# A fused attention and mixer kernel: stores of r two ticks later, five w2 tiles spread over the second pass, words of the head's conversions at other places

## The chip, the cores and the metric

The kernel runs on one core of one Trainium2 chip. The metric is the device time of one execution in microseconds; lower is better. All times of before come from three timed runs and from one profiled execution.

## What is computed

The reference is a linear attention with decay, whose output x (4 batches, 768 positions, 512 columns) goes through a low-rank mixing over positions and a two-layer channel product:

```python
h = xt @ U @ V                                     # xt = x transposed, rank 32
u = x + h.transpose(0, 2, 1)
ch = np.maximum(u @ w_ch1, 0.0) @ w_ch2            # 512 -> 2048 -> 512
return (u + ch).astype(np.float32)
```

The attention walks over blocks of 64 positions with a 64x64 state for each of 32 heads. The change does not touch it. The weights U, V, w_ch1 and w_ch2 come as 64-bit numbers, that is as pairs of 32-bit words; the kernel makes fp32 numbers of them.

## The kernel before, in words

The work runs in five parts. TensorE multiplies numbers in the form fp32r, which keeps fewer bits than fp32, so every operand is split into a high and a low part, and a product is made of three matmuls: high by high and low by low (or a near relative of these) into one accumulator, and a third with sums of the parts into another or the same one, with scales that bring the pieces together.

1. **The attention** for 24 blocks of 128 positions, with its products, the low-rank mixing and the transposes into columns u.
2. **The head of the first product** (`hidden`, lines 889 to 906): four units, each a pair of groups of 512 rows by one tile of 128 of the 2048 hidden columns. A unit has 16 matmuls of high and low parts, 8 of the third part, two evacuations by ScalarE (L896), two sums by VectorE (L905) and two stores of r (L906). Between its matmuls other pieces are placed by number: `(unit, n, what)` means "ahead of matmul n of this unit". Among them are mixings (`mix`, whose sum x_nat is L626), transposes of the last six blocks (`turn`, L659), and the steps that convert words to weights.
3. **The single units** (`run_unit`): the first four groups by the other tiles, with 8 + 4 matmuls each. Beside them run the conversions of w1 and w2 tiles, strewn over the units by tables (`strew`: this step after that unit). Sums and differences of w1 halves are made here and stored as `forms_d`.
4. **The second pass** of the first product: the last two groups. For the tile pairs 1 to 7 it multiplies seven forms instead of eight (`seven_of`, a scheme of Strassen's kind); pair 0 takes the plain eight (`eight_of`). Its order is `sequence`, 53 forms; after the high pieces of a form stands a `tick`, at which the steps strewn over the tick numbers run. A block of seven ticks belongs to one pair. A form takes six matmuls. The weights come as a stream: for every two forms a load of `forms_d` (L1088), the high part on ScalarE (L276), the low part on VectorE (L279), the third on GpSimd (L285). Results r are taken from the accumulators by ScalarE (L1197), summed by VectorE (L1193) and stored by `give` (L1201).
5. **The second product**: relu(r) is split into three parts m (`split`, L1306 ScalarE, L1307 and L1308 VectorE) after a load (`fetch`, L1300), and multiplied with the 16 tiles of w2 (L1322, L1324, L1326). A w2 tile is prepared by `w2_split` with the steps load, high, low, third. The first four tiles get their own buffers (`e`) and are made during the second pass, with the third part on GpSimd; the others are made at the beginning of the second product, with low (L267) and third (L270) on VectorE, into buffers that the first product has left.

What sets the order: each engine takes its instructions in program order, and up to the end of the second pass that order is written out by hand (`manual_schedule`); what follows `ordered.close()` is placed by the framework, and may begin between the last pieces of the second pass. All loads and stores of the parts 2 to 5 are issued by one queue, SP, which waits in its order, too: a store that waits for a sum holds the loads behind it.

Converting a tile of w1 has eight steps: fetch the words (L149; one buffer in the head, three later), `one` (L170 on VectorE, then L177 and L178 on ScalarE), `two` (L188), `three` (L196, the last reader of the words), `four` (L201), `five` (L231, ScalarE), `six` (L234) and `seven` (L239, both VectorE). In the head `second` and `third` are these steps for the w1 tiles 2 and 3.

Of the kernel before, what the change touches and what calls it, by code (L numbers as in the profile page):

```python
# [18 lines left out]
def kernel(  # L19
# [28 lines left out]
    nc = tc.nc  # L48
# [7 lines left out]
    FT = FF // P  # L56
# [46 lines left out]
    r_d = [[dram.tile([P, N], FP32, name=f"r_d{ft}_{g}") for g in range(NG)] for ft in range(FT)]  # L103
    w2_d = [dram.tile([P, C], FP32, name=f"w2_d{ft}") for ft in range(FT)]
    forms_d = [dram.tile([P, 8, C // 2], FP32, name=f"forms_d{j}") for j in range(FT // 2)]
# [119 lines left out]
    def w1_steps(ft, in_parts=False, apart=False):  # L225
        st = {}

        def five():
            w1v[ft] = o = w_tile(ft)
            st["t"], st["p"] = o[:, 0, :].bitcast(FP32), w1_plain[ft]  # L230
            on_scalar(lambda: nc.scalar.mul(o[:, 0, :], st["p"], NEAR))  # L231

        def six():
            nc.vector.tensor_tensor(  # L234
                out=w1v[ft][:, 1, :], in0=st["p"], in1=st["t"], op=ALU.subtract
            )

        def seven():
            nc.vector.scalar_tensor_tensor(  # L239
                w1v[ft][:, 2, :], st["t"], -E, w1v[ft][:, 1, :].bitcast(FP32), ALU.mult, ALU.add  # L240
            )

        cols = moe_w_ch1[:, ft * P : (ft + 1) * P].rearrange("(c p) f -> p c f", p=P)
        return weight_steps(plain(w1_plain, ft), cols, C, in_parts=in_parts, apart=apart) + [
            five, six, seven,
        ]
# [77 lines left out]
    raw = {}  # L324
# [68 lines left out]
    st = {}  # L393
# [305 lines left out]
    for s in range(NS):  # L699
        b, c = divmod(s, NT)  # L700
# [5 lines left out]
        step = [("fade", s)] * (c > 0)  # L706
# [82 lines left out]
    side = {}  # L789
# [51 lines left out]
    last = side.pop(NS)  # L841
# [33 lines left out]
    def hidden(ft, pair, before={}):  # L875
# [35 lines left out]
    rest = [  # L911
        (0, 4, "enter", None),
        (0, 7, "turn", c0 - 2), (0, 9, "low", b), (0, 14, "low_rows", b),
        (0, 14, "next_of_low", b), (0, 14, "next_of_low", b), (0, 14, "next_of_low", b),
        (0, 15, "turn", c0 - 1), (0, 22, "mix", c0),
    ]

    at = [(1, 5), (1, 17), (2, 4), (2, 17), (3, 3), (3, 10)]
# [5 lines left out]
    head = [(pair, ft) for ft in (0, 1) for pair in pairs]  # L924
    third, second = w1_steps(3), w1_steps(2)
    run["do"] = lambda step: step()
    side = [(0, step) for step in last[4:] + second[:1]] + [(1, third[0])]
    places = (1, 8), (1, 9), (1, 20), (1, 21), (1, 23), (2, 7), (2, 8), (2, 20), (2, 21)
    places += (3, 12), (3, 13), (3, 14)
    rest += [(*place, "do", step) for place, step in zip(places, second[1:] + third[1:])]  # L930
    for i, (pair, ft) in enumerate(head):
        before = {}
        for unit, n, *piece in rest:
# [11 lines left out]
    ]  # L945
    HC = C // 2
    SEVEN = (1, 2, 3, 4, 5, 6, 7)
    LAST = FT - 4


    one = iter(range(1 << 30))
# [59 lines left out]
    def form_steps(j):  # L1011
        st = {}
        f, f2 = 2 * j, 2 * j + 1

        def some(a, b, out):
            def step():
                if "t" not in st:
                    st["t"] = sums_pool.tile([P, 4, HC], FP32, tag="t", name="t")
                    w, w2 = w1_plain[f], w1_plain[f2]
                    st["b"] = [w[:, 0:HC], w2[:, 0:HC], w[:, HC:], w2[:, HC:]]  # L1020
                at = [st["t"][:, i] for i in range(4)] + st["b"]
                nc.vector.tensor_tensor(out=at[out], in0=at[a], in1=at[b], op=ALU.subtract)

            return step

        def keep():
            for i, w in enumerate((w1_plain.pop(f), w1_plain.pop(f2))):
                nc.sync.dma_start(
                    out=forms_d[j][:, 2 * i : 2 * i + 2], in_=w.rearrange("p (c f) -> p c f", c=2)
                )  # L1030
            if st:
                nc.sync.dma_start(out=forms_d[j][:, 4:8], in_=st["t"])

        if j not in SEVEN:
            return [keep]
        return [some(5, 4, 0), some(7, 5, 2), some(7, 0, 1), some(6, 1, 3), keep]
# [4 lines left out]
    at = {}  # L1041

    def strew(units, steps):
        assert len(units) == len(steps)
        for n, step in zip(units, steps):
            at.setdefault(n, []).append((units[0], step))
# [1 line left out]
    def after(n, offsets):  # L1048
        return [max(0, n + i) for i in offsets]

    strew((0, 2), third[6:])
    FIRST, W1 = (-3, 0, 0, 2, 2, 2, 4, 4), (-3, 0, 1, 2, 2, 3, 5, 5)
    W2 = (-3, 0, 1, 2, 2, 3)
    strew((1, 1, 2, 2, 2), form_steps(1))
# [8 lines left out]
    for j, n in ((2, 9), (3, 16), (4, 21), (5, 28), (6, 34), (7, 38)):  # L1063
        strew((n, n, n + 1, n + 1, n + 1) if j in SEVEN else (n,), form_steps(j))
    units = [(g, ft) for ft in range(2, LAST) for g in range(FG)]
    units += [(g, ft) for g in range(FG) for ft in range(LAST, FT)]

    sequence = []
# [10 lines left out]
    for n in range(0, len(sequence), 2):  # L1079
# [6 lines left out]
        def fetch(w, n=n):  # L1086
            for i, (j, form) in enumerate(sequence[n : n + 2]):
                nc.sync.dma_start(out=w[:, i * HC : (i + 1) * HC], in_=forms_d[j][:, form])  # L1088
# [5 lines left out]
    places, form_of = {}, {}  # L1094
# [69 lines left out]

    def forms_made():
        whole_ctx.close()
        e_pool.append(ctx.enter_context(tc.tile_pool(name="e", bufs=4, reuse_waits="tile")))

    e_pool, ticks = [], iter(range(1 << 30))

    def tick():
        for what in late[1:]:
            what()
        late[1:] = []
        for began, step in sorted(at.pop(next(ticks), ()), key=lambda what: what[0]):
            step()

    def weights_of(key):
# [19 lines left out]
        return t  # L1198

    def give(t, ft, g):  # L1200
        nc.sync.dma_start(out=r_d[ft][g], in_=t)  # L1201

    def both(z, d):
        t = taken(z, 4096.0 + 1.0)
# [3 lines left out]
    def seven_of(j, ends):  # L1208
# [5 lines left out]
        def on_chain(i, of):  # L1214
            add_up(z, high_pieces((j, i), of), False)
            tick()
            add_up(d, third_pieces((j, i), of), False)

        add_up(z, high_pieces((j, 0), "a11"), True)
        tick()  # L1220
        one_two = next_bank("c11", rest)
        nc.scalar.copy(one_two, z)
# [26 lines left out]
        give(c12, f2, g0)  # L1249
        add_to(c22, five)  # L1250
        give(c22, f2, g1)

        def end():
# [48 lines left out]
    def split(i):  # L1302
        r = rs.pop(i)
        ms[i] = m = m_pool.tile([P, 3, N], F32R, tag="m", name="m")
        hi, low = m[:, 0].bitcast(FP32), m[:, 1].bitcast(FP32)
        nc.scalar.activation(out=m[:, 0], in_=r, func=AF.Relu, scale=NEAR)  # L1306
        nc.vector.scalar_tensor_tensor(m[:, 1], r, 0.0, hi, ALU.max, ALU.subtract)  # L1307
        nc.vector.scalar_tensor_tensor(m[:, 2], hi, E, low, ALU.mult, ALU.subtract)  # L1308
# [19 lines left out]
    def residual(g):  # L1328

        for n in range(TG):  # L1330
            if n % 3 == 0:
                t = w1_pool.tile([P, 3, C], F32R, tag="w1", name="u").bitcast(FP32)
            us[n] = t[:, n % 3, :]
            nc.sync.dma_start(out=us[n], in_=u_d[g * TG + n])
# [20 lines left out]
    def ahead(i):  # L1355
        if i + 3 < len(steps):
            fetch(i + 3)
        if i + 2 < len(steps):
            split(i + 2)
# [4 lines left out]
    def w2_split(ft):  # L1364
        def raw():
            t = e_pool[0].tile([P, 3, C], F32R, tag="e", name="w2")
            w2t[ft] = [t[:, i, :] for i in range(3)]
            return w2t[ft][2].bitcast(FP32)

        if ft >= 4 and ft % 4 == 0:  # L1370
            hl = hl_pool.tile([P, 4, 2, C], F32R, tag="hl", name="w2_hl")
            d = d_pool.tile([P, 4, C], F32R, tag="d", name="w2_d")
            for i in range(4):
                w2t[ft + i] = [hl[:, i, 0], hl[:, i, 1], d[:, i]]
        return divided_steps(
            lambda: w2t[ft], lambda w: nc.sync.dma_start(out=w, in_=w2_d[ft]),
            nc.gpsimd if ft < 4 else nc.vector,
            ft < 4, raw,
        )

    def begin_second():
# [6 lines left out]
    assert not later  # L1388
    total = len(sequence)
    strew((total - 14,), [begin_second])  # L1390
    for ft in range(4):
        strew(
            (total - 24 + 5 * ft, total - 20 + 5 * ft, total - 19 + 5 * ft, total - 18 + 5 * ft),
            w2_split(ft),
        )
    for n in range(3):
        strew((total - 5 + n,), [lambda n=n: fetch(n)])
    for n in range(2):
        strew((total - 2 + n,), [lambda n=n: split(n)])
    pending = []  # L1400
    for j in range(FT // 2):
        (seven_of if j in SEVEN else eight_of)(j, pending)
    for end in pending:
        end()
    assert not at
    ordered.close()
    spare = 1

# [1 line left out]
    for i in range(len(steps) - STAG):  # L1410
        g, ft = steps[i]
        ahead(i)
        if i + 4 < FT:
            for step in w2_split(i + 4):
                step()
        if i == len(steps) - STAG - 1:
            ahead(i + 1)
        if ft == FT - STAG - 1:
            residual(g)
        for n in range(TG):  # L1420
            product(i, n)
        del ms[i]
        if ft == FT - 1:
            for n in range(TG):
                finish(g, n)
# [36 lines left out]
```

## Time and profile before

| what | value |
|---|---|
| time, median of 3 runs | 649.32 us (649.31 to 651.44) |
| the profiled execution's own time | 648.26 us |
| its span | 646.5 us |
| TensorE clock granted | 1.00 |
| VectorE, ScalarE and GpSimd busy | 71%, 51% and 22% of the span |
| moved by DMA | 129.74 MB, 201 GB/s on average |

In time, the attention takes the span up to about 114 us, the head of the first product to 146, the single units to about 300, the second pass to about 378, and the second product the rest. In the rows that follow, an order of time gives start and duration in us, engine, line, operation, what it writes and reads, shapes, and in brackets the engine's idle time before it and what ended it. A row of waits gives the total in us, how many times, and the longest. A row of stretches gives the limits, the length, then for each engine asked for its busy time and instructions, the granted clock, the busy share of the DMA engines and GB/s. PE is TensorE, PEld its weight load, DVE VectorE, ACT ScalarE, POOL GpSimd, SPq the queue of SP. A matmul is listed with 389 ns, but matmuls overlap, and the next one starts earlier.

### The profile page before, as it was taken

How to read it: one execution, taken by the hardware profiler on the slowest of the kernel's cores; microseconds unless marked ns; L12 is line 12 of the kernel's file. 1: busy time of each engine (PE TensorE's matmuls, PEld its weight loads, DVE VectorE, ACT ScalarE, POOL GpSimd, SP SyncE). 2: the span in 40 equal slices, each digit the busy share in tenths (PEclk: the TensorE clock that was granted, in tenths of full speed). 3: DMA queues.
4: the chain of work that ended last, by engine and by line, in shares of the span. 5: the costliest groups of instructions: out<-in, count | busy, mean ns of one | idle time of the engine just before them, and what ended most of it. 6: DMA issues, size and time to landing. Idle time of an engine off the chain costs nothing.

```text
span 646.5 us, 13608 instructions
## 1 busy us (share of the span) xinstructions
PE 633.1 (98%) x5200; PEld 529.9 (82%) x5200; DVE 461.3 (71%) x739; ACT 331.7 (51%) x607; POOL 144.9 (22%) x123
## 2 busy tenths in 40 slices
PE   9999999989999999999999999999999999999997
PEld 8889989768888888887888768888888888888886
DVE  6766878566878788788677899785575665755854
ACT  3676766354777777777667654232322322322320
POOL 4475978000000000000355630030030300300300
PEclk9999999999999999999999999999999999999999
DMA  9989995347888898664567589353363353442521
GB/s 216 253 203 264 225 250 156 128 166 276 295 297 292 283 320 300 250 211 170 178 208 232 202 295 327 120 191 127 101 220 100 127 197 98 170 156 98 179 82 65
DMA packets 141379, 129.74 MB, mean 201 GB/s; under 512 B 82498, under 2 KB 98498, under 8 KB 141314
## 3 DMA queue, kind: packets, MB, share of 16 engines
q1 hardware_dynamic: 116192, 122.45, 58.6%
q10 hardware_dynamic: 25122, 6.42, 4.4%
q8 instruction: 41, 0.67, 0.4%
q14 instruction: 24, 0.20, 0.1%
HBM read 78.64 MB, written 49.81 MB: 199 GB/s over the span
## 4 chain that ended last, share of the span: by engine, by line
PE 90%; DMA 4%; DVE 2%; ACT 2%; issue 1%; ACTq 0%; SPq 0%; DVEq 0%
PE pz L959 25%; PE pz L1324 13%; PE pz L1322 13%; PE pd L1326 13%; PE px L514 4%; PE pss L463 4%; PE z L959 3%; PE p L959 2%; PE px L525 2%; PE pqk L416 2%; PE d L959 2%; DMA words<-in_moe_w_ch_dram 2%; PE pkv L486 1%; PE c L959 1%; PE pm L618 1%
## 5 line engine op out<-in xcount | busy, mean ns | idle before, releaser
L1306 ACT ACTIVATE m<-rm 128x512 fp32r<-128x512 f32 x96 | 60.6, 631 | 169.0 <-PE pd L1326 130.8
L1307 DVE SCALAR_TENSOR_TENSOR m<-rm,m 128x512 fp32r<-128x512 f32 x96 | 71.5, 745 | 81.7 <-ACT m L1306 81.7
L1322 PE MATMUL pz<-w_hl,m 128*128 128x512 f32 x288 | 112.0, 389 | 0.0
L1324 PE MATMUL pz<-w_hl,m 128*128 128x512 f32 x288 | 112.0, 389 | 0.0
L1326 PE MATMUL pd<-w_d,m 128*128 128x512 f32 x288 | 110.7, 389 | 0.0
L959 PE MATMUL pz<-u_hl,w 128*128 128x512 f32 x448 | 110.3, 389 | 0.0
L959 PEld LDWEIGHTS pz<-u_hl,w 128*128 128x128 f32 x448 | 84.1, 188 | 17.4
L285 POOL TENSOR_TENSOR w<-w 128x512 fp32r<-128x512 f32 (+1 forms) x27 | 38.2, 1430 | 225.1 <-DVE w L279 216.0
L1308 DVE SCALAR_TENSOR_TENSOR m<-m 128x512 fp32r<-128x512 f32 x96 | 74.5, 777 | 2.6
L1351 POOL TENSOR_TENSOR o<-o,u 128x512 f32<-128x512 f32 x20 | 29.8, 1519 | 196.7 <-DVE o L1347 196.7
L1322 PEld LDWEIGHTS pz<-w_hl,m 128*128 128x128 f32 x288 | 54.1, 188 | 11.3
L1326 PEld LDWEIGHTS pd<-w_d,m 128*128 128x128 f32 x288 | 54.1, 188 | 11.2
L1324 PEld LDWEIGHTS pz<-w_hl,m 128*128 128x128 f32 x288 | 54.0, 188 | 11.2
L959 PE MATMUL pz<-u_d,w 128*128 128x512 f32 x224 | 59.7, 389 | 0.0
L966 ACT ACTIVATE pz<-pz 128x512 f32<-128x512 f32 x60 | 34.9, 581 | 28.6 <-PE pz L959 27.5
L959 PEld LDWEIGHTS pz<-u_d,w 128*128 128x128 f32 x224 | 42.0, 188 | 8.7
L472 DVE TENSOR_TENSOR sm<-pss,mask 128x512 f32<-128x512 f32 x48 | 30.9, 685 | 18.5 <-PE pss L463 18.3
L970 ACT ACTIVATE r<-pz 128x512 f32<-128x512 f32 x60 | 35.7, 596 | 14.3 <-PE pz L959 13.1
L196 DVE SCALAR_TENSOR_TENSOR sc<-words,sc 128x512 uint32<-128x512 uint32 (+2 forms) x34 | 24.0, 705 | 21.2 <-ACT sc L178 21.2
L1322 PE MATMUL pz<-w,m 128*128 128x512 f32 x96 | 37.3, 392 | 0.4 <-DVE r L1193 0.3
L1324 PE MATMUL pz<-w,m 128*128 128x512 f32 x96 | 36.9, 392 | 0.0
L1326 PE MATMUL pd<-w,m 128*128 128x512 f32 x96 | 36.5, 390 | 0.2 <-DVE m L1308 0.2
(143 smaller groups left out, 1100.0 us busy)
## 6 DMA issues: line engine op xcount, KB each, us to landing
r_d<-r SPq DMA_DIRECT2D x96, 256.0 KB, 2.6
rm<-r_d SPq DMA_DIRECT2D x96, 256.0 KB, 2.6
words<-in_moe_w_ch_dram SPq DMA_DIRECT2D x30, 512.0 KB, 4.7
wf<-forms_d SPq DMA_DIRECT2D x53, 128.0 KB, 3.0
u_d<-x_nat SPq DMA_DIRECT2D x24, 256.0 KB, 4.0
u<-u_d SPq DMA_DIRECT2D x24, 256.0 KB, 4.3
qraw<-in_q_dram SPq DMA_DIRECT2D x23, 256.0 KB, 4.7
out_dram<-o SPq DMA_DIRECT2D x23, 256.0 KB, 2.0
```

Of the source, the lines that this page charges most:

```text
L285: engine.tensor_tensor(out=st["third"], in0=st["low"].bitcast(FP32), in1=st["hi"].bitcast(FP32), op=ALU.subtract,)
L472: nc.vector.tensor_tensor(out=sm[:, x], in0=pss[:, x], in1=mask[:, x], op=ALU.mult)
L959: nc.tensor.matmul(out=out, lhsT=weights, rhs=moving, start=start and i == 0, stop=i == len(pieces) - 1, skip_group_check=not start,)
L966: nc.scalar.mul(acc, acc, 1.0 + E)
L970: nc.scalar.mul(r, acc, 4096.0)
L1306: nc.scalar.activation(out=m[:, 0], in_=r, func=AF.Relu, scale=NEAR)
L1307: nc.vector.scalar_tensor_tensor(m[:, 1], r, 0.0, hi, ALU.max, ALU.subtract)
L1308: nc.vector.scalar_tensor_tensor(m[:, 2], hi, E, low, ALU.mult, ALU.subtract)
L1322: nc.tensor.matmul(out=pz, lhsT=m[:, 0, cols], rhs=hi, start=first, stop=False)
L1324: nc.tensor.matmul(out=pz, lhsT=m[:, 1, cols], rhs=low, start=False, stop=end)
L1326: nc.tensor.matmul(out=pd, lhsT=m[:, 2, cols], rhs=third, start=first, stop=end)
L1351: nc.gpsimd.tensor_tensor(out=o, in0=o, in1=u, op=ALU.add)
```

## The change

- In the head, tile 2's words are fetched ahead of matmul 5 of unit 0 instead of after unit 0, and tile 3's ahead of matmul 22 of unit 1 instead of after unit 1. Tile 2's other steps stay. Tile 3's step `one` goes from (2, 20) to (3, 12), `two` from (2, 21) to (3, 13); `three`, `four` and `five` go from unit 3 to the first single unit, `six` from the first to the third single unit.
- `keep` doesn't store the first half of the second tile of the pairs that use seven forms (this form is not read again).
- `give` strews the store of r two ticks on, except where the sequence ends before.
- Five w2 tiles instead of four are made early, with load, high, low and third in the ticks n, n+4, n+5 and n+6, where n is 6, 13, 20, 27 and 34; before, n was 29, 34, 39 and 44. The buffers `e` are five. In the second product eleven tiles are left to make instead of twelve, and each is prepared five steps ahead instead of four.
- The first three loads of r for the second product are placed four ticks sooner, in the ticks 44 to 46, and the first two splits in 49 and 51 instead of 51 and 52.

```diff
-    side = [(0, step) for step in last[4:] + second[:1]] + [(1, third[0])]
-    places = (1, 8), (1, 9), (1, 20), (1, 21), (1, 23), (2, 7), (2, 8), (2, 20), (2, 21)
-    places += (3, 12), (3, 13), (3, 14)
-    rest += [(*place, "do", step) for place, step in zip(places, second[1:] + third[1:])]
+    side = [(0, step) for step in last[4:]]
+    places = (0, 5), (1, 8), (1, 9), (1, 20), (1, 21), (1, 23), (2, 7), (2, 8)
+    places += (1, 22), (3, 12), (3, 13)
+    rest += [(*place, "do", step) for place, step in zip(places, second + third)]
...
-    LAST = FT - 4
+    LAST, EARLY = FT - 4, 5
...
             for i, w in enumerate((w1_plain.pop(f), w1_plain.pop(f2))):
+                a = 1 if st and i else 0
                 nc.sync.dma_start(
-                    out=forms_d[j][:, 2 * i : 2 * i + 2], in_=w.rearrange("p (c f) -> p c f", c=2)
+                    out=forms_d[j][:, 2 * i + a : 2 * i + 2],
+                    in_=w.rearrange("p (c f) -> p c f", c=2)[:, a:],
                 )
...
-    strew((0, 2), third[6:])
+    strew((0, 0, 0, 2, 2), third[3:])
...
-        e_pool.append(ctx.enter_context(tc.tile_pool(name="e", bufs=4, reuse_waits="tile")))
+        e_pool.append(ctx.enter_context(tc.tile_pool(name="e", bufs=EARLY, reuse_waits="tile")))
...
-        for began, step in sorted(at.pop(next(ticks), ()), key=lambda what: what[0]):
+        at["now"] = now = next(ticks)
+        for began, step in sorted(at.pop(now, ()), key=lambda what: what[0]):
             step()
...
     def give(t, ft, g):
-        nc.sync.dma_start(out=r_d[ft][g], in_=t)
+        n = at["now"] + 2
+        step = lambda: nc.sync.dma_start(out=r_d[ft][g], in_=t)
+        strew((n,), [step]) if n < len(sequence) else step()
...
-        if ft >= 4 and ft % 4 == 0:
+        if ft >= EARLY and (ft - EARLY) % 4 == 0:
...
-            for i in range(4):
+            for i in range(min(4, FT - ft)):
...
-            nc.gpsimd if ft < 4 else nc.vector,
-            ft < 4, raw,
+            nc.gpsimd if ft < EARLY else nc.vector,
+            ft < EARLY, raw,
...
-    for ft in range(4):
-        strew(
-            (total - 24 + 5 * ft, total - 20 + 5 * ft, total - 19 + 5 * ft, total - 18 + 5 * ft),
-            w2_split(ft),
-        )
+    for ft in range(EARLY):
+        n = 6 + 7 * ft
+        strew((n, n + 4, n + 5, n + 6), w2_split(ft))
     for n in range(3):
-        strew((total - 5 + n,), [lambda n=n: fetch(n)])
+        strew((total - 9 + n,), [lambda n=n: fetch(n)])
     for n in range(2):
-        strew((total - 2 + n,), [lambda n=n: split(n)])
+        strew((total - 4 + 2 * n,), [lambda n=n: split(n)])
...
-        if i + 4 < FT:
-            for step in w2_split(i + 4):
+        if i + EARLY < FT:
+            for step in w2_split(i + EARLY):
                 step()
```

More of the change, by code (lines that the diff above doesn't have):

```diff
@@ L1404 @@
         end()
-    assert not at
+    assert list(at) == ["now"]
     ordered.close()
```

## The prediction

> **What bounds the kernel now.** I read the busy shares first, then TensorE by stretches, then its waits, then the order of time around them.
>
> ```profile
> span 646.5 us, 13608 instructions
> PE 633.1 (98%) x5200; PEld 529.9 (82%) x5200; DVE 461.3 (71%) x739; ACT 331.7 (51%) x607; POOL 144.9 (22%) x123
> ```
> ```profile
> 146.48:300.61 154.13, 154.13 (x681) 1.00 0.80 276
> 300.61:303.99 3.38, 3.01 (x13) 1.00 0.70 239
> 303.99:361.27 57.28, 57.28 (x254) 1.00 0.59 196
> 361.27:387.47 26.20, 24.42 (x98) 1.00 0.78 259
> 387.47:620.00 232.53, 232.53 (x1027) 1.00 0.46 157
> ```
>
> TensorE is busy for 98% of the span, so a change that leaves the matmuls alone can win only its gaps. The stretch rows give length, TensorE's busy time and its matmuls (one that began before the stretch is counted, so I take one off each). Where there is no gap, a matmul starts every 154.13/680 = 0.2267 or 232.53/1026 = 0.2266 us. The stretch from 361.27 to 387.47, the end of the second pass and the start of the second product, holds 97 matmuls that need 97 x 0.2267 = 22.0 us, and takes 26.2: **4.2 us lost**. From 300.61 to 303.99 some 0.5 us is lost to an evacuation that the diff leaves alone.
>
> The other gaps within reach lie at the head of the first product:
>
> ```profile
> PE pz L889 <- ACT r L896: 1.6, 1, 1.6
> PE put L659 <- DVE x_nat L626: 1.3, 1, 1.3
> ```
> ```profile
> 129.54:131.42 1.88, 0.23 (x2) 1.00 0.02 8
> 131.42:141.28 9.86, 9.86 (x49) 1.00 0.50 161
> 141.28:142.82 1.54, 0.29 (x2) 1.00 0.31 114
> ```
>
> The first and third stretch run from where the next matmul was due to where it started: 1.88 + 1.54 = **3.4 us lost**. So 4.2 + 3.4 = 7.6 us, 1.2% of the time, is the most that is to be had.
>
> **The head: words sooner.** Rows picked from the order of time of VectorE, SP and ScalarE:
>
> ```profile
> 115.11 0.68 DVE L196 SCALAR_TENSOR_TENSOR sc<-words,sc 128x512 uint32<-128x512 uint32 x1
> 124.40 0.46 SPq L149 DMA_DIRECT2D words<-in_moe_w_ch_dram  x1
> 128.94 0.43 DVE L170 TENSOR_SCALAR sc<-words 128x512 uint32<-128x512 uint32 x1 [3.75 <-DMA words<-in_moe_w_ch_dram]
> 130.79 1.07 ACT L896 ACTIVATE r<-pz 128x512 f32<-128x512 f32 x2
> ...
> 134.00 0.41 SPq L149 DMA_DIRECT2D words<-in_moe_w_ch_dram  x1
> 139.39 0.43 DVE L170 TENSOR_SCALAR sc<-words 128x512 uint32<-128x512 uint32 x1 [2.82 <-DMA words<-in_moe_w_ch_dram]
> 140.80 1.28 DVE L905 SCALAR_TENSOR_TENSOR r<-pd,r 128x512 f32<-128x512 f32 x2
> ```
>
> The fetch of tile 2's words stands on SP behind unit 0's r stores, issues at 124.40 and lands 4.5 us later. The conversion is queued on VectorE and ScalarE ahead of the evacuations L896; these start at 130.79, and unit 2, which needs their banks, waits. Tile 3's words issue at 134.00, land 5.4 us later and hold L905 and a sum behind it; a transpose waits.
>
> Placed ahead of matmul 5 of unit 0, the first fetch waits only for the single words buffer, free when L196 ends at 115.79. Even at 5.4 us it lands by 121.2. Its reader's place (1, 8) is 16 matmuls, 3.6 us, ahead of the unit's end at 129.54: some four microseconds to spare. Late next is L896 itself: its matmuls end eight before the unit's end, at 127.7, and it takes 1.07, so 128.8, before unit 2 is due. The second fetch, at (1, 22), needs tile 2's L196 at (1, 20), done by about 129.3, and lands by 134.7; its reader moves to (3, 12), 2.7 us ahead of the end of unit 3, past 140. Both waits go. On SP the fetches are moved ahead of r and u_d stores that nobody awaits here.
>
> Tile 3's steps three to five move into the first single unit and six into the third: two VectorE instructions of 0.7 us there, and one each of ScalarE and VectorE. In the unit's time VectorE is busy 5.97 of 9.52 us:
>
> ```profile
> 146.48:156.00 9.52, 9.52 (x44) 7.88 (x42) 5.97 (x12) 3.13 (x6) 0.00 (x0) 1.00 0.82 282
> ```
>
> (PE, PEld, DVE, ACT, POOL.) The tile is multiplied from the fifth unit on, about 9 us later, so this costs nothing; without that cover it would be 1.4 us. The head gives between 1.5 (one wait stays) and 3.4; with cover on both sides I take **-3.3**.
>
> **Stores of r asked later.** SP takes its queue in order:
>
> ```profile
> 355.84 4.51 SPq L1201 DMA_DIRECT2D r_d<-r  x3
> 360.44 0.91 SPq L1088 DMA_DIRECT2D wf<-forms_d  x2
> ...
> 364.26 0.63 ACT L276 ACTIVATE w<-wf 128x512 fp32r<-128x512 f32 x1 [2.22 <-DMA wf<-forms_d]
> 365.43 1.20 PE L959 MATMUL z<-s_hl,w 128*128 128x512 f32 x4 [0.46 <-ACT r L1197]
> ...
> 365.41 0.69 DVE L1193 SCALAR_TENSOR_TENSOR r<-d,r 128x512 f32<-128x512 f32 x1 [2.51 <-ACT r L1197]
> ```
>
> Three stores hold SP for 4.51 us until VectorE has finished their tiles; two weight loads queue behind them, ScalarE waits 2.22 us for the landing, its evacuation of z is late, TensorE loses 0.5 us and VectorE idles 2.51. A tick is six matmuls, 1.36 us; asked two ticks later, the stores come behind the loads of those ticks. No wait is added, but an r tile is held 2.7 us longer:
>
> ```profile
> r_d<-r SPq DMA_DIRECT2D x96, 256.0 KB, 2.6
> ```
>
> With four tiles made in seven ticks (9.5 us), seven buffers come round in 16.7 us. The longest held, c11, is made in the first tick of its block, asked in the eighth and landed 2.6 us later: 12.1 us. The cover is 4.6 us; without it ScalarE would wait to take z, and TensorE behind it, which is not in the sum.
>
> The Trainium skill (DMA: Bandwidth & Descriptors, "Issuing engines are not separate DMA queues") counts the time to initiate a DMA as usually small beside the transfer. By that alone, three stores out of the way would be worth three short issues; the 4.51 us row differs, because the waits are served in the queue too.
>
> **Five early w2 tiles, spread out.** VectorE is the second limit where the pass ends:
>
> ```profile
> 305.00:325.00 20.00, 12.71 (x17) 1.00 0.52 169
> 325.00:345.00 20.00, 13.61 (x21) 1.00 0.64 214
> 345.00:365.00 20.00, 16.93 (x23) 1.00 0.69 229
> 365.00:385.00 20.00, 19.48 (x28) 1.00 0.74 250
> 385.00:411.00 26.00, 26.00 (x45) 1.00 0.81 275
> ```
> ```profile
> L279 DVE SCALAR_TENSOR_TENSOR w<-w x4: 681/1094/1778, 352.1 to 373.9; 128x512 fp32r<-128x512 f32 x4
> ```
> ```profile
> 366.87 1.31 POOL L285 TENSOR_TENSOR w<-w 128x512 fp32r<-128x512 f32 x1 [1.57 <-DVE w L279]
> ```
>
> From 365 to 411 VectorE has almost no idle time. It makes the low pieces of the four early tiles (the group, 681 to 1778 ns each) in ticks 34, 39, 44 and 49; changed, those of five tiles in 11, 18, 25, 32 and 39. Three more fall into the time before 345, where VectorE has 7.3 + 6.4 us idle. Of the crowded stretch two go (2 x 1.1 to 2 x 1.78 us), the idle 2.51 comes back, and tile 4's low and third piece (0.7 us each at least) move to tick 39 and to GpSimd: 6 us or more of relief against the 4.2 lost. The loads of 256 KB, five for four, are moved on SP to ticks 6 to 34, under half a microsecond of issue each.
>
> Do the early pieces find room? In the fourth block:
>
> ```profile
> 338.79 0.57 ACT L1222 COPY c<-z 128x512 f32<-128x512 f32 x1 [0.69 <-PE z L959]
> ```
> ```profile
> 341.78 0.69 DVE L1193 SCALAR_TENSOR_TENSOR r<-d,r 128x512 f32<-128x512 f32 x1 [0.90 <-ACT r L1197]
> ```
>
> Each block puts ScalarE's 0.63 us ahead of this copy and VectorE's 0.68 ahead of this sum: the idle 0.69 and 0.90 take them. GpSimd, which is idle 1.57 us before the row above, makes five third pieces of 1.31 us for four. I cost all this at nothing; without the cover, contended, at five times 1.1 us (1.78 less 0.68).
>
> The m tiles' loads four ticks sooner and their splits up to two ticks sooner touch the last part of the 4.2. The store of half a tile less per block saves 128 KB seven times on a queue that does not bind: nothing. Where the 4.2 lie:
>
> ```profile
> 361.27:377.53 16.26, 15.16 (x64) 1.00 0.74 248
> 377.53:387.47 9.94, 9.26 (x36) 1.00 0.84 278
> ```
>
> One matmul taken off each, 16.26 - 63 x 0.2267 = 2.0 us before the first matmul of the second product and 9.94 - 35 x 0.2267 = 2.0 after it (the remaining 0.2 is the count at the border). The first part is that of the late loads and the late VectorE, and I expect all but 0.4 of it. Of the second I expect two thirds, since m still passes through ScalarE and twice VectorE before its first use. The pass gives between 0 and 4.2; I take **-3.0**.
>
> **Sum.** -3.3 - 3.0 = -6.3. The profiled execution took 648.26 (span 646.5 and 1.8 around it), 1.1 under the median of 649.32; I take the difference off the median: **643.0 us**.
>
> **Rivals.**
> *One half only.* The pass stays bound by VectorE, whose work is moved and not removed: -3.3, 646.0. Or the head's gaps are taken by the next wait: -3.0, 646.3. For the first speaks the full VectorE after 385; against it, the idle room before 345.
> *No visible change.* The orders differ and SP still waits as long, since buffers, not the stores, hold the loads: within 1.5 us, about 648.5. Against it: L196 frees its buffer 8.6 us before the fetch.
> *Slower.* The early pieces delay the stream's weights. A low piece takes VectorE 1.78 us instead of 0.68 where GpSimd works beside it; if the stream's next piece is late by more than the 0.9 us of room, TensorE waits up to 1.78 in each of five blocks, 8.9 us, the end stays as it was, and 649.3 - 3.3 + 8.9 = 654.9. It decides at 3.3/5 = 0.7 us a block. The Trainium skill (GPSIMD Engine Reference, "Key points") has a rule for it: GpSimd shares its SBUF interfaces with VectorE and contends with instructions of two SBUF inputs. The group of 681 to 1778 ns agrees. Against it: the idle time in the rows above.
>
> **How the numbers follow.** Forecast 0.65 (641.3 to 645), one half 0.20 (645 to 647), no visible change 0.09, slower 0.06. Half a per cent, 3.2 us, is about what a measurement tells: the limit is 646.1. Half of the second case lies below it, and a sixth of the slower case within half a per cent: faster 0.75, same 0.20, slower 0.05. The range reaches from nearly all of both losses, 641.0, into the second case, 646.8.
>
> **What would show it.** The waits of pz on L896 and of put on x_nat are gone, and the words issue near 116 and 128. No triple of stores holds SP for 4 us; ScalarE waits under 1 us for stream weights; VectorE idles again before 385; the 97 matmuls take 23 to 24 us. It would be wrong if gaps appear between 303 and 361, where there are none now, or if L1193 waits for an r buffer.

## The result and the profile after

The median of the changed kernel's runs is 643.55 us, beside 650.0 for the kernel before in the same comparison: ratio 0.9903 (95% interval 0.9881 to 0.9924), or 6.3 us less. Two later comparisons of the same kernel gave 0.9922 (0.9898 to 0.9947) and 0.9919 (0.9889 to 0.9948), 5.1 and 5.3 us. The profiled execution took 643.46 us (before: 648.26). The ratios here and below leave out three slow executions: 656.08 us of pass_only, 1044.66 us of early_only and 1262.86 us of w2_by_hand. Busy times by engine, from the page after:

```profile
span 641.6 us, 13618 instructions
PE 632.1 (99%) x5200; PEld 530.3 (83%) x5200; DVE 464.5 (72%) x738; ACT 331.9 (52%) x607; POOL 147.8 (23%) x124
```

The spans differ by 4.9 us. The stretches of the changed kernel (limits, length, busy PE, PEld, DVE, ACT, POOL, granted clock, DMA share, GB/s) tell where:

```profile
112.04:141.19 29.15, 29.15 (x188) 23.48 (x183) 17.92 (x34) 15.42 (x29) 0.66 (x1) 1.00 0.46 163
141.19:295.33 154.14, 154.14 (x682) 127.63 (x680) 125.23 (x220) 113.55 (x189) 0.00 (x0) 1.00 0.78 270
...
298.72:336.85 38.13, 38.13 (x169) 31.53 (x168) 30.90 (x41) 27.81 (x50) 17.88 (x13) 1.00 0.61 200
336.85:369.64 32.79, 32.75 (x141) 25.97 (x140) 27.58 (x38) 21.82 (x40) 23.73 (x16) 1.00 0.76 244
369.64:378.00 8.36, 6.99 (x22) 4.83 (x21) 7.12 (x13) 5.46 (x10) 0.00 (x0) 0.80 0.88 310
```

The head begins at 112.04 instead of 113.97, with no instruction changed ahead of it: 1.9 us by chance. It takes 29.15 us instead of 32.51: **3.36 us gained, with no gap left**. The single units take what they took (154.1). But from the first form of the seven-form blocks to the end of the program, the kernel before took 646.5 - 309.45 = 337.05 us and the changed one 641.6 - 304.19 = 337.41. **In this execution the second pass gained nothing.** What it wins by 369 it loses in the next 8.36 us, where only 21 or 22 matmuls run, some at a granted clock below 1.

The head, in the order of time of SP, VectorE and ScalarE:

```profile
113.88 0.38 SPq L149 DMA_DIRECT2D words<-in_moe_w_ch_dram  x1
...
123.21 0.42 DVE L170 TENSOR_SCALAR sc<-words 128x512 uint32<-128x512 uint32 x1
...
125.39 1.09 ACT L896 ACTIVATE r<-pz 128x512 f32<-128x512 f32 x2 [0.25 <-PE pz L889]
...
126.49 0.38 SPq L149 DMA_DIRECT2D words<-in_moe_w_ch_dram  x1
```

The words are issued 9.3 us ahead of L170, which begins without a wait, and L896 now waits for its matmuls, not for the conversion. Both fetches came as soon as L196 was done (113.86 and 126.46), as forecast.

The loss at the change of products, as ScalarE's order of time shows it, and two of TensorE's waits:

```profile
367.68 0.59 ACT L1200 ACTIVATE r<-z 128x512 f32<-128x512 f32 x1
370.04 1.29 ACT L266 ACTIVATE w_hl<-wf 128x512 fp32r<-128x512 f32 x2 [1.77 <-DMA wf<-w_d]
371.23 0.58 ACT L966 ACTIVATE p<-p 128x512 f32<-128x512 f32 x1
371.75 1.13 ACT L1311 ACTIVATE m<-rm 128x512 fp32r<-128x512 f32 x2
372.79 0.57 ACT L1200 ACTIVATE r<-z 128x512 f32<-128x512 f32 x1
```
```profile
PE z L959 <- ACT r L1200: 0.8, 1, 0.8
PE p L959 <- ACT p L966: 0.6, 1, 0.6
```

The high parts of w2 tiles 5 and 6 (L266) stand in ScalarE's queue ahead of the scaling of p (L966), and wait 1.77 us for their load; then two high parts of m (L1311) stand ahead of the evacuation of z (L1200). TensorE waits for p, and then for z. Behind these gaps the clock falls to half (TensorE's stretches, the granted clock in the column behind the count):

```profile
372.00:374.00 2.00, 1.19 (x4) 0.98 0.75 253
374.00:376.00 2.00, 2.00 (x6) 0.50 0.81 277
376.00:378.00 2.00, 2.00 (x7) 0.66 0.96 320
```

Two microseconds at full clock hold nine or ten matmuls; here six and seven.

### The profile page after: what moved, and what is told of

Its sections match the earlier page's. It is cut to its first block, busy times and chain, and to the rows that moved or that the text cites. A ratio compares the mean times of both kernels' runs of the same rounds, so it can differ in the third digit from the quotient of the medians.

```text
span 641.6 us, 13618 instructions
## 1 busy us (share of the span) xinstructions
PE 632.1 (99%) x5200; PEld 530.3 (83%) x5200; DVE 464.5 (72%) x738; ACT 331.9 (52%) x607; POOL 147.8 (23%) x124
## 4 chain that ended last, share of the span: by engine, by line
PE 94%; ACT 2%; DMA 2%; SPq 1%; issue 1%; DVE 0%; ACTq 0%; DVEq 0%
PE pz L959 25%; PE pz L1327 14%; PE pz L1329 14%; PE pd L1331 13%; PE px L514 4%; PE z L959 4%; PE pss L463 3%; PE p L959 3%; PE pz L889 2%; PE px L525 2%; PE d L959 2%; PE pqk L416 2%; PE pkv L486 1%; PE c L959 1%; PE pd L900 1%; PE pm L618 1%
## 5 line engine op out<-in xcount | busy, mean ns | idle before, releaser
L1311 ACT ACTIVATE m<-rm 128x512 fp32r<-128x512 f32 x96 | 60.5, 631 | 176.7 <-PE pd L1331 145.8
L959 PE MATMUL pz<-u_hl,w 128*128 128x512 f32 x448 | 110.3, 389 | 0.0
L1327 PE MATMUL pz<-w_hl,m 128*128 128x512 f32 x264 | 102.7, 389 | 0.0
L1329 PE MATMUL pz<-w_hl,m 128*128 128x512 f32 x264 | 102.7, 389 | 0.0
L1331 PE MATMUL pd<-w_d,m 128*128 128x512 f32 x264 | 101.4, 389 | 0.0
L959 PEld LDWEIGHTS pz<-u_hl,w 128*128 128x128 f32 x448 | 84.1, 188 | 17.4
L285 POOL TENSOR_TENSOR w<-w 128x512 fp32r<-128x512 f32 (+1 forms) x28 | 41.6, 1510 | 215.0 <-DVE w L279 202.4
L959 PE MATMUL pz<-u_d,w 128*128 128x512 f32 x224 | 59.7, 389 | 0.0
L1331 PEld LDWEIGHTS pd<-w_d,m 128*128 128x128 f32 x264 | 49.6, 188 | 10.4
L1327 PEld LDWEIGHTS pz<-w_hl,m 128*128 128x128 f32 x264 | 49.6, 188 | 10.2
L1329 PEld LDWEIGHTS pz<-w_hl,m 128*128 128x128 f32 x264 | 49.6, 188 | 10.2
L959 PEld LDWEIGHTS pz<-u_d,w 128*128 128x128 f32 x224 | 42.0, 188 | 8.8
L966 ACT ACTIVATE pz<-pz 128x512 f32<-128x512 f32 x60 | 34.9, 581 | 27.3 <-PE pz L959 27.3
L1329 PE MATMUL pz<-w,m 128*128 128x512 f32 x120 | 47.2, 393 | 0.0
L1327 PE MATMUL pz<-w,m 128*128 128x512 f32 x120 | 47.0, 393 | 0.0
L1331 PE MATMUL pd<-w,m 128*128 128x512 f32 x120 | 46.8, 391 | 0.0
L196 DVE SCALAR_TENSOR_TENSOR sc<-words,sc 128x512 uint32<-128x512 uint32 (+2 forms) x34 | 24.3, 713 | 21.2 <-ACT sc L178 21.2
```

Source lines behind the costliest of these rows:

```text
L285: engine.tensor_tensor(out=st["third"], in0=st["low"].bitcast(FP32), in1=st["hi"].bitcast(FP32), op=ALU.subtract,)
L959: nc.tensor.matmul(out=out, lhsT=weights, rhs=moving, start=start and i == 0, stop=i == len(pieces) - 1, skip_group_check=not start,)
L966: nc.scalar.mul(acc, acc, 1.0 + E)
L1327: nc.tensor.matmul(out=pz, lhsT=m[:, 0, cols], rhs=hi, start=first, stop=False)
L1329: nc.tensor.matmul(out=pz, lhsT=m[:, 1, cols], rhs=low, start=False, stop=end)
L1331: nc.tensor.matmul(out=pd, lhsT=m[:, 2, cols], rhs=third, start=first, stop=end)
```

## The experiments

Each was timed in five rounds beside the kernel before. The two stretches are from one profiled execution each: the head from the first L889 to the first L959; "pass to end" from the first form of the seven-form blocks to the end of the span.

| kernel | ratio to before (95% interval) | head, us | pass to end, us |
|---|---|---|---|
| before, first profile | | 32.51 | 337.05 |
| before_again | 1.0022 (0.9998 to 1.0046) | 35.03 | 337.55 |
| head_only | 0.9953 (0.9927 to 0.9979) | 29.15 | 339.28 |
| stores_only | 0.9953 (0.9925 to 0.9981) | 35.14 | 333.47 |
| early_only | 0.9985 (0.9960 to 1.0009) | 35.27 | 336.52 |
| pass_only | 0.9969 (0.9942 to 0.9996) | 32.16 | 335.36 |
| after, first profile | 0.9903 (0.9881 to 0.9924) | 29.15 | 337.41 |
| after_again | 0.9922 (0.9898 to 0.9947) | 29.14 | 339.93 |
| after_third | 0.9919 (0.9889 to 0.9948) | 29.17 | 335.40 |
| w2_load_sooner | 0.9891 (0.9848 to 0.9934) | 29.13 | 335.43 |
| w2_by_hand | 0.9925 (0.9897 to 0.9954) | 29.14 | 336.51 |
| head_and_stores | 0.9881 (0.9841 to 0.9921) | 29.13 | 333.43 |
| m_at_old_ticks | 0.9864 (0.9827 to 0.9902) | 29.16 | 333.83 |
| m_sooner_old_tiles | 0.9907 (0.9879 to 0.9936) | 29.17 | 335.85 |

Where the times differ from the sum of the two stretches, it is the front: over these fourteen profiles the head began anywhere from 112.04 to 117.98 us. The single units took 156.48 or 156.49 us in all of them, counted to the first s_d matmul.

**The two kernels again.** No edit was made.

before_again: 

> The kernel before, unchanged, as a second profile and as a measure of chance. Every theory: ratio 1.000 within 0.003. The first profile's front, up to the first unit of the head, ended at 113.97 us, that of the changed kernel at 112.04, with no instruction changed there: if this is chance in the input transfers, the front of this profile lies anywhere between 111.5 and 114.5. If it is a trait of the kernel before, it lies at 114 again.

after_again: 

> The changed kernel, unchanged, as a second profile. Ratio 0.988 to 0.992 by every theory. Theory A (forecast: head -3.3 and pass -3.0): the stretch from the start of the second pass to the end of the program is some 3 us shorter than before's 343.5. Theory B (read from the first profile after): that stretch is as long as before, since ScalarE's early high parts of the w2 tiles wait for their load at the change of products, TensorE stands for about 2 us there and then runs some matmuls at a reduced clock; gaps of 0.5 us or more again near 372, granted clock below 1 there.

after_third: 

> The changed kernel once more, beside the three others on one chip. Start of the second pass to the end 337 to 340 us with the gap of p or z at the change of products, ratio 0.990 to 0.993, so slower than head and stores alone by 0.2 to 0.4%.

The front of before_again began its head at 112.96: chance, not a trait. But its head took 35.03 us, 2.5 more than the first profile's, and its TensorE waits show that the second wait is not of one size:

```profile
PE put L659 <- DVE x_nat L626: 2.3, 1, 2.3
PE pz L889 <- ACT r L896: 1.5, 1, 1.5
```

The longer wait is only part of the 2.5 us. Behind it the clock was granted at half:

```profile
144.00:146.00 2.00, 2.00 (x6) 0.50 0.52 194
```

From the end of that wait to the first L959 it took 5.23 us, where the first profile took 3.66 at full clock: 1.6 us of the 2.5 are the clock, about 1.1 the longer wait, less 0.1 at the other wait. Stores_only and early_only, with waits of 2.15 and 2.23 us at this place, show the same.

Theory A, the forecast, expected the pass to end 3 us shorter. It ended at 337.41, 339.93 and 335.40, beside 337.05, 337.55 and 339.28 with the old pass: theory B was the nearer one. The gap was there each time; L266 waited 1.77, 3.09 and 1.18 us. In after_third, where it waited least, the clock stayed at 1.00 and the stretch was the shortest. A gap of 0.81 us at z came each time; the gap at p was 0.56 us, 1.86 us and none that the profile lists.

**The halves apart.** head_only has the diff's lines from `side` to `rest` and the `strew` of `third`; pass_only has all the others.

head_only: 

> The kernel before with the head's part of the change alone. Both theories: head 29.1 us instead of 32.5, so -3.4 us, ratio 0.9948. A rival, that the single units or the second pass give the time back: ratio above 0.998.

pass_only: 

> The changed kernel with the head as before. Theory A: -3.0 us, ratio 0.9954. Theory B: between -0.5 and +0.5 us, ratio 0.9992 to 1.0008, and the gap at the change of products is in its profile.

The head alone gives 3.1 us by the times, near the 3.4 of both theories. The pass gives 0.9969, 2.0 us, between the two, and its interval (0.3 to 3.8 us) reaches into both; its profile has the gap at z, 0.81 us, and none at p (L266 waited 1.37 us).

**The pass's parts.** stores_only is before with the two-tick `give` (and the line of `tick` that keeps the tick's number):

```diff
     def give(t, ft, g):
-        nc.sync.dma_start(out=r_d[ft][g], in_=t)
+        n = at["now"] + 2
+        step = lambda: nc.sync.dma_start(out=r_d[ft][g], in_=t)
+        strew((n,), [step]) if n < len(sequence) else step()
```

> The kernel before with the stores of r asked two ticks later, alone. Theory A: the triple store no longer holds SP for 4 us, ScalarE waits under 1 us for stream weights, -1 us or a little more, ratio 0.998 to 0.9985. Rival: the loads are then held by their buffers (SP waits for the low part L279 instead), and the time stays: ratio 0.9995 to 1.001.

early_only is before with five tiles at the new ticks (and the shorter store of `keep`):

```diff
-    for ft in range(4):
...
+    for ft in range(EARLY):
+        n = 6 + 7 * ft
+        strew((n, n + 4, n + 5, n + 6), w2_split(ft))
```

> The kernel before with five early w2 tiles spread over the second pass, alone; stores, m and the head as before. Theory A: VectorE is relieved at the end of the pass, -1 to -2 us, ratio 0.997 to 0.9985. Theory B: ScalarE waits for the load of tile 5 at the change of products here too, ratio 0.999 to 1.002.

The stores alone brought 0.9953 and the shortest stretch so far, 333.47: three times what was expected of them. By this stretch that is more than the whole pass brought; by the times (0.9953 and 0.9969) the intervals overlap. The early tiles alone: 0.9985, an interval that holds 1. What SP waits for, between 300 and 390 us, first before, then in stores_only:

```profile
SPq L1201 <- DVE r L1193: 29.9, 25, 3.2
SPq L971 <- ACT r L970: 8.9, 6, 3.1
SPq L1300 <- DVE m L1307: 3.8, 5, 1.4
SPq L1088 <- DVE w L279: 1.0, 3, 0.4
```
```profile
SPq L1088 <- DVE w L279: 19.3, 14, 3.7
SPq L971 <- ACT r L970: 11.1, 7, 3.1
SPq L1203 <- DVE r L1194: 6.3, 11, 2.6
```

The queue is held for almost as long, but by its loads, which wait for a free buffer, and so as early as they can be; the stores (L1201, later L1203) wait 6.3 us instead of 29.9. ScalarE's wait for stream weights, between 300 and 390 us before and in early_only, and between 300 and 380 in stores_only:

```profile
ACT w L276 <- DMA wf<-forms_d: 6.5, 5, 2.2
```
```profile
ACT w L276 <- DMA wf<-forms_d: 8.1, 7, 2.2
```
```profile
ACT w L276 <- DMA wf<-forms_d: 1.0, 3, 0.4
```

The spread tiles leave that wait standing (8.1 us), the stores take it away (1.0). And VectorE, which I had taken for the second limit? The last 24 us of 78 from the first seven-form block, before, in stores_only, in the first profile after and in m_at_old_ticks (below):

```profile
363.45:387.45 24.00, 22.30 (x90) 15.95 (x89) 21.93 (x32) 15.24 (x28) 10.41 (x8) 1.00 0.78 263
```
```profile
366.93:390.93 24.00, 24.00 (x106) 19.28 (x105) 22.31 (x36) 13.66 (x26) 10.59 (x8) 1.00 0.86 291
```
```profile
358.19:382.19 24.00, 22.63 (x89) 17.39 (x89) 19.78 (x31) 12.54 (x24) 8.05 (x6) 0.93 0.86 292
```
```profile
359.47:383.47 24.00, 24.00 (x105) 19.28 (x104) 19.86 (x33) 12.93 (x25) 7.57 (x6) 1.00 0.83 270
```

With the stores later, TensorE runs 106 matmuls without a gap while VectorE is busy for 22.31 of 24 us, with the old tiles at their old ticks. So a VectorE that is this full was not the limit. That its lateness came from the late loads is shown for the first gap, where ScalarE waited 2.22 us for a load and VectorE 2.51 us for ScalarE; for the later gaps it is inferred from their absence here.

**Against the gap at the change of products.** Two attempts. w2_load_sooner asks tile 5's and 6's loads by hand:

```diff
...
+    for ft in (5, 6):
+        strew((46,), [lambda ft=ft: load_sooner(ft)])
...
```

> The changed kernel, with the loads of w2 tiles 5 and 6 asked by hand in tick 46, ahead of the stores of r of that tick; their high parts stay where the framework puts them on ScalarE. Theory B (the gap at the change of products is ScalarE waiting for this load, ahead of the evacuations in its queue): no wait of L266 for wf, no gap of p behind L966, clock 1.00 there, start of the second pass to the end 334 to 335 us instead of 337.4 and 339.9, ratio to the kernel before 0.986 to 0.989. Rival C (VectorE or the DMA engines bound that stretch, and the wait only shows it): another wait takes the place, ratio 0.990 to 0.993.

w2_by_hand keeps the first four steps of the second product in the order written by hand:

```diff
-    ordered.close()
...
+        if i == 4:
+            ordered.close()
```

> The changed kernel, with the first four steps of the second product still in the order that is written by hand, so that ScalarE's high parts of w2 tiles 5 to 8 stand behind the last evacuations. Theory B: as with the loads sooner, ratio 0.986 to 0.989. Rival C: 0.990 to 0.993. If the framework's mixing of the two products is worth more than the wait costs, the ratio is above 0.993.

Neither settled it. In w2_load_sooner the load was still late, as ScalarE's order of time shows:

```profile
370.50 1.27 ACT L266 ACTIVATE w_hl<-wf 128x512 fp32r<-128x512 f32 x2 [1.40 <-DMA wf<-w_d]
```

so that it was not the test it was meant to be; its 0.9891 has an interval that holds every theory. In this profile, too, the gap at z is 0.81 us, as in the three of the changed kernel and in pass_only, whatever L266 waits (1.18 to 3.09 us): behind L266 the scaling of p, two high parts of m and the evacuation of z follow each other on ScalarE without a break. So these profiles don't part the load's share in that gap from m's. In w2_by_hand p and z were not held, but the stretch, 336.51, was no better; other waits came (one of TensorE's and one of ScalarE's between 280 and 400 us):

```profile
PE pz L1329 <- DVE m L1312: 0.8, 1, 0.8
```
```profile
ACT w_hl L266 <- DMA wf<-w_d: 9.5, 5, 6.8
```

**Which edit makes the gap.** Three kernels on one chip, with after_third. head_and_stores has only these two parts; m_at_old_ticks is the changed kernel with the loads and splits of m put back; m_sooner_old_tiles is head_and_stores with m sooner:

```diff
-        strew((total - 5 + n,), [lambda n=n: fetch(n)])
+        strew((total - 9 + n,), [lambda n=n: fetch(n)])
...
-        strew((total - 2 + n,), [lambda n=n: split(n)])
+        strew((total - 4 + 2 * n,), [lambda n=n: split(n)])
```

head_and_stores: 

> The kernel before with two parts of the change alone: the head, and the stores of r two ticks later (four early tiles at their old ticks, m at its old ticks). From the runs so far: head 29.15 us, start of the second pass to the end 333.5 us, ratio about 0.9953 x 0.9953 = 0.9906 by the medians, 0.989 by the stretches. If the stores' gain seen alone was chance, that stretch is 337 us again and the ratio 0.995.

m_at_old_ticks: 

> The changed kernel with the loads and splits of m at their old ticks (head, stores and five spread tiles as changed). Theory D (the sooner m work puts ScalarE's high parts of tiles 5 and 6, which wait for their load, ahead of the last evacuations): here they stand behind the evacuation p in the queue, no wait at the change of products, start of the second pass to the end 333.5 to 334.5. Theory E (the five spread tiles crowd VectorE and GpSimd): 335.5 us or more.

m_sooner_old_tiles: 

> Head, stores and the sooner m loads and splits, with four early tiles at their old ticks. Theory D: the gap at the change of products is there, start of the second pass to the end 335 to 338 us. Theory E: 333 to 334 us.

The two with m at its old ticks took 333.43 and 333.83 from the pass to the end, the two with m sooner 335.85 and 335.40. So the sooner m costs the time, with the old tiles as with the new, as theory D had it. Theory E falls: the spread tiles cost 0.4 us in these profiles, which is no difference to speak of. But the mechanism of theory D, evacuations held on ScalarE, is not what stopped TensorE in m_sooner_old_tiles. Its wait there, and VectorE's order of time:

```profile
PE d L959 <- DVE r L1194: 2.0, 2, 1.6
```
```profile
375.22 1.65 DVE L1311 SCALAR_TENSOR_TENSOR m<-m 128x512 fp32r<-128x512 f32 x1
376.80 0.68 DVE L1194 SCALAR_TENSOR_TENSOR r<-d,r 128x512 f32<-128x512 f32 x1
```

TensorE waits for the sum L1194. By the rows its last input came from ScalarE's L1198, which ended at 373.60 (below), but the sum stands behind two pieces of m (L1310 and L1311) in VectorE's queue. The sooner m held a sum on VectorE here, and evacuations on ScalarE in the changed kernel. In head_and_stores TensorE's only wait from 280 to 400 us is the one that the diff leaves alone:

```profile
PE pz L959 <- ACT pz L966: 0.4, 1, 0.4
```

ScalarE's order of time, m_sooner_old_tiles first, then stores_only, which has m at its old ticks, then before:

```profile
373.01 0.59 ACT L1198 ACTIVATE r<-z 128x512 f32<-128x512 f32 x1
375.80 0.63 ACT L266 ACTIVATE w_hl<-wf 128x512 fp32r<-128x512 f32 x1 [2.21 <-DMA wf<-w_d]
376.34 0.58 ACT L966 ACTIVATE p<-p 128x512 f32<-128x512 f32 x1
376.86 1.13 ACT L1309 ACTIVATE m<-rm 128x512 fp32r<-128x512 f32 x2
```
```profile
377.20 0.58 ACT L966 ACTIVATE p<-p 128x512 f32<-128x512 f32 x1 [0.76 <-PE p L959]
377.70 0.62 ACT L1309 ACTIVATE m<-rm 128x512 fp32r<-128x512 f32 x1
379.02 0.60 ACT L1198 ACTIVATE r<-z 128x512 f32<-128x512 f32 x1 [0.70 <-PE z L959]
379.51 1.14 ACT L1309 ACTIVATE m<-rm 128x512 fp32r<-128x512 f32 x2
380.61 0.63 ACT L266 ACTIVATE w_hl<-wf 128x512 fp32r<-128x512 f32 x1
```
```profile
374.65 0.63 ACT L266 ACTIVATE w_hl<-wf 128x512 fp32r<-128x512 f32 x1 [0.17 <-DMA wf<-w_d]
375.43 0.58 ACT L966 ACTIVATE p<-p 128x512 f32<-128x512 f32 x1
```

With the stores late and m at its old ticks (stores_only, head_and_stores, m_at_old_ticks), p and z come first and L266 behind them; with the stores late and m sooner, the framework places L266 ahead of p, and more high parts of m ahead of z. But with the stores at their old place L266 stands ahead of p as well, with m at its old ticks: in before, before_again, head_only and early_only, where it waited 0.17, 0.21, 1.82 and 0.32 us. So the later stores do two things, they let the loads pass and they move L266 behind p, and no run parts the two. Why the framework decides so was not tried.

By the ratios the best kernel is m_at_old_ticks, 0.9864, with head_and_stores at 0.9881 beside it; after_third on the same chip had 0.9919. Their intervals overlap, so that the times alone don't show the order; the stretches do, by 1.5 us and more, each from one execution: 333.43 to 333.83 in the three profiles with late stores and old m, 335.36 to 339.93 in the six that have the sooner m and the framework's own order.

## Why the prediction came out right, point by point

The forecast was 643.0 us and -6.3; measured were 643.55 and ratios that make -5.1 to -6.3. The total was right, one of its two terms for its own reason, the other only in part. That the first comparison met the 6.3 so closely was luck: of the 4.9 us between the two first profiles 1.9 lie in the front, where no instruction changed, 3.4 in the head, and the pass took 0.4 back.

- **The head, -3.3: right, mechanism and size.** 32.51 became 29.15. Every profile with the new places has 29.13 to 29.17 and no wait there; with the old ones it took 32.16 to 35.27. What I took for the most that was to be had, 3.4 us, was the loss of one execution: the second wait ran from 0.8 to 2.3 us over the five profiles with the old places, and in the three where it passed 2 us the clock fell to half behind it. The gain by the profiles differs with them (3.0 to 6.1 us).
- **Stores of r: mechanism right, size too small.** I gave them no term of their own and left the larger share of the -3.0 to VectorE's relief. Alone they take 3.6 us off the stretch from the pass to the end (337.05 to 333.47), nearly all of the 4.2 lost there, and 0.9953 by the time. A part of this may be the order at the change of products, which they alter too. The buffers for r did not run out.
- **Five early tiles: "6 us or more of relief against the 4.2 lost" failed.** The relief came (VectorE busy 19.86 of the last 24 us instead of 22.31), and the early pieces found their room, as TensorE's busy 38.13 of 38.13 us shows. But the relief bought nothing: 333.83 with it, 333.43 without. Of the sign that I had named, the 97 matmuls in 23 to 24 us, nothing came in the first profile after: they took 26.0 us. A full engine in the window of the gaps was no proof that it caused them.
- **m sooner: the step "touch the last part of the 4.2" failed, with its sign.** I counted a gain; it costs 1.6 to 2.4 us beside kernels that differ in it alone (335.40 and 335.85 against 333.83 and 333.43), and up to 6.1 where the load lands late and the clock falls. I had looked only at what m itself waits for, not at what it would push back in the queues of ScalarE and VectorE, the last evacuations and sums.
- **The sum.** Stores -3.6, m and its consequences from +1.6 to +6: that nets to -2.0 at best, and the time of pass_only says -2.0, a microsecond short of the forecast, though its interval holds the -3.0 too. With the head's -3.1 this makes -5.1, about what the two later comparisons measured (-5.1 and -5.3); the first comparison made up the rest by chance.
- **The rivals.** "One half only" describes the first profile (-3.36 and +0.36), though not by the reason given for it, a pass bound by VectorE. "Buffers, not the stores, hold the loads" was half true: SP waits 18 to 19 us for buffers now, but early, and ScalarE waits only 0.6 us for stream weights. "Slower" did not show: from 298.72 to 369.64 TensorE was busy for all but 0.04 us, although the low pieces beside GpSimd took up to 1.8 us. The Trainium skill (GPSIMD Engine Reference, "Key points") names this contention with VectorE instructions of two SBUF inputs, and the low pieces have two.

## What to carry to other kernels

On a queue that takes its entries in order, ask a store only when its data is nearly due, and let the loads pass first: here that one edit was worth 3.6 us where 4.2 us were lost. Before giving a full engine relief, look for what made it late; here VectorE had stood idle for 2.51 us just ahead of its full stretch, waiting for a load by way of ScalarE. A change that starts work sooner must be read in every queue that it shifts, and where a framework orders the work, in the order that it makes of it, since an evacuation or a sum that stands behind other work stops TensorE.

## What the hardware showed that I had not expected

Gaps of one or two microseconds were followed by half the clock on TensorE. In the first profile after, two gaps of 0.56 and 0.81 us within 3 us were followed by 2 us at 0.50 and 2 at 0.66; in after_again gaps of 1.86 and 0.81 us were followed by more than 4 us at 0.50:

```profile
376.00:378.00 2.00, 0.73 (x2) 0.91 0.56 175
378.00:380.00 2.00, 1.53 (x4) 0.50 0.65 190
380.00:382.00 2.00, 2.00 (x6) 0.50 0.99 318
382.00:384.00 2.00, 2.00 (x6) 0.50 1.01 365
```

The Trainium skill (TensorE: Matmul & The Clock Gate, "What's actually happening") names an idle window of about 3.4 us ahead of the lower clock; the longest gap behind which the clock fell here is 2.34 us. The length of one gap doesn't decide it. In the head with the old places, gaps of 2.15, 2.23 and 2.34 us were followed by 0.50, gaps of 0.78 and 1.26 us by 1.00. During the attention, gaps of 1.98 us (m_sooner_old_tiles) and 2.22 us (w2_by_hand) were followed by 0.50, one of 2.00 us (after_again) by 1.00; the first two are the executions whose head began last, at 117.82 and 117.98. In m_sooner_old_tiles the gap of 1.58 us at the change of products left the clock at 1.00. What decides it stays open. So such a gap costs its own length in one execution and more in another: 1.6 us more in before_again's head, and in the first profile after, by 2 us at 0.50 and 2 at 0.66, an estimated 1.7. This is part of why the changed kernel's stretch varied from 335.4 to 339.9 us.
